# Two score blocks under way on VectorE, and 196 blocks in place of 172, in a gated mix of two attentions

## The chip, the cores and the metric

The kernel runs on one core of a Trainium2 chip. The metric is the device time of one execution in microseconds (us). The engines of a core work side by side, each through a queue of its own in program order: TensorE (PE, matmuls), VectorE (DVE), ScalarE (ACT), GpSimd (POOL) and SyncE (SP, which issues DMAs).

## The reference

For `x` of 2048 x 512 (bf16), two attentions are computed and mixed by a gate per row. A is full attention with 32 heads of 16; B looks at 8 earlier rows, two apart.

```python
g = sigmoid((x * gate_w).sum(-1, keepdims=True))
# A: full attention
q, k, v = split(x @ wqkv)                       # 32 heads of 16
p = softmax(einsum("bhqd,bhkd->bhqk", q, k) * 16 ** -0.5)
a = einsum("bhqk,bhkd->bhqd", p, v).merge_heads() @ wo
# B: the same, but each query sees rows s, s-2, ..., s-14 only (masked below 0)
b = local_attention(x, B_wqkv, B_wo)
out = g * a + (1 - g) * b
```

## The kernel before

**Full attention (A).** The work is cut into 32 periods, each one of 4 chunks of 512 queries and one of 8 groups of four heads. The periods run over the chunks in pairs: first all groups of the chunks 0 and 1, then those of 2 and 3. A period has 64 score blocks, 16 tiles of 128 keys for each of four heads; a block has 128 keys by 512 queries. TensorE computes the scores into PSUM (`qk`, tile `ring`), ScalarE exponentiates two or three blocks by one instruction (`ex`, from `ring` into `pT`), and TensorE multiplies them with the values and accumulates (`pv`, tile `acc`). A column of ones beside the values gives the sum for the division. At the end of a period VectorE transposes `acc` (`accT`), takes the reciprocal (`rden`), and GpSimd divides.

**Blocks on VectorE.** In each period the first `n_dve[pi]` blocks of the list `dorder` (the last two key tiles) are not given to ScalarE: VectorE computes an approximate exponential with integer arithmetic on the bits. These are 172 of 2048 blocks. `d_group` makes them, two by two. For each block `chain_of` issues `dq` (two matmuls into one bank `misc`: a constant term from `off`, then the scores) and four passes over 128 x 512 on VectorE: `p1` writes `dt` from the scores, `p2` and `p3` write `dt` again from the scores and `dt`, `p4` writes the result into `pd`. Then `pv` of the group multiplies both blocks with the values. There is one buffer `dt`, so that a block's four passes come to an end before the next block's first. `pd` holds two blocks, with three buffers. The matmuls `dq` of a block come after the start of the last pass (`d_last`) of the block before.

**PSUM.** `ring` has two sets of banks (three and two). Three banks, `misc0` to `misc2`, serve everything else: the accumulators, all projections, the outputs and the blocks for VectorE.

**Around it.** TensorE also does the projections of A, period by period, and those of B; VectorE evacuates them. Attention B runs mostly on GpSimd, from tiles that DMAs fetch with shifted rows. `zero` issues matmuls with zeros (`z`, tile `z32`) into `acc`, which change no sum and fill TensorE's gaps.

**What sets the order.** Every step is an `Op` with an engine, an assumed duration `occ`, a due time `dl`, its predecessors (`deps` wait for an end, `after` for a start) and the buffers it takes and uses (`tok`). `list_schedule` plays the steps through and always takes, of those that can start on an engine, the one with the earliest due time; `AHEAD` says how far it looks past the first, and `slack` is a margin that it leaves behind a step of VectorE or GpSimd before TensorE or GpSimd uses the result. The steps are then issued in that order, engine by engine, and keep it on the chip. `CFG` holds the parameters; the due times of a period come from `S0 = T0 + UNIT * (blocks before it)`. Nearly all instructions are recorded by one helper, so the profile has one line for them (L285, matmuls L297) and they are told apart by their tiles.

Of the kernel before, what the change touches and what calls it, by code (L numbers as in the profile page):

```python
# [9 lines left out]
ALU = mybir.AluOpType  # L10
# [3 lines left out]
U16 = mybir.dt.uint16  # L14
# [2 lines left out]

CFG = dict(
    set_sizes=(3, 2),
    n_dve=(3,) * 2 + (5,) * 14 + (6,) * 16,  # L20
    dve_tiles=2,
    p_bufs=4,
    pairs=True,
    cover=0.68,
    force=1.0,
    d_slack=2.0,
    d_lead=4.0,
    d_early=5.0,
    dq_early=10.0,
    d_late=8.0,  # L30
    pd_bufs=3,
    q_bufs=3,
    shift=6.0,
    hold=0.3,
    pv_dl=2.2,
    first=0.0,
    same=2.0,
    step=2,
    early=0.25,
    a_slack=0.6,  # L40
    v_slack=0.3,
    g_slack=4.0,
    unit=0.461,
    t0=18.5,
    b_start=32.0,
    b_space=46.7,
    chain=("pe", "dve", "act", "pool", "sp"),
)
# [58 lines left out]
class Op:  # L107

    def __init__(self, eng, occ, fn, dl, deps=(), alloc=(), use=(), lat=None, rel=0.0, name="",
                 after=(), rows=False, cover=None, slack=None, sums=()):  # L110
        self.eng, self.occ, self.fn, self.dl, self.rel, self.name = eng, occ, fn, dl, rel, name
        self.rows, self.zeros, self.spare = rows, 0, None
        self.sums = sums
        self.slack = {"dve": CFG["v_slack"], "pool": CFG["g_slack"]}.get(eng, 0.0) if slack is None else slack
        self.cover = cover if cover is not None else (occ if not callable(occ) else 0.0)
        self.after = [d for d in after if d is not None]
        self.deps, self.alloc = [d for d in deps if d is not None], list(alloc)
        self.lat = (occ if not callable(occ) else occ(0.0)) + LAT[eng] if lat is None else lat
        self.done = None
        for tk in list(alloc) + list(use):  # L120
            tk.ops.append(self)
# [3 lines left out]
WAVE = lambda n: 0.01 + 0.205 * n  # L125
TURN = 0.10
SPAN, COVER, ZERO = 3.41, CFG["cover"], 0.216
AHEAD = dict(pe=0.10, dve=0.12, act=0.25, pool=0.5, sp=0.0)


def list_schedule(ops, spare):
# [23 lines left out]
    while len(out) < len(ops):  # L155
        best = None
        for e, cs in cand.items():
            if not cs:
                continue
            es = [(max(free[e], avail(o)), o) for o in cs]  # L160
            t0 = min(x[0] for x in es)
            if t0 < INF and (best is None or t0 < best[0]):
                best = (t0, e, es)
        if best is None:
            raise RuntimeError("no op can start: " + ", ".join(o.name for cs in cand.values() for o in cs))
        t0, e, es = best
        same = CFG["same"] if e == "pe" else 0.0
        t, o = min(((t, o) for t, o in es if t <= t0 + AHEAD[e]),
                   key=lambda x: (x[1].dl - (same if x[1].rows == rows else 0.0), x[0]))
        if e == "pe" and not o.name.startswith("qk"):  # L170
            nxt = min(((ts, x) for ts, x in es if x.name.startswith("qk") and ts < t0 + CFG["hold"]), default=None,
                      key=lambda x: x[0])
            if nxt is not None:
                due = max(nxt[0], free["act"] - nxt[1].lat - CFG["early"])

                def ends(t, x):
                    return t + x.occ + (TURN if x.rows != rows else 0.0) + (0.0 if x.rows else TURN)
                if ends(t, o) > due + 0.03:
                    fits = [(t, x) for t, x in es if t <= t0 + AHEAD[e] and ends(t, x) <= due + 0.03]
                    t, o = min(fits, key=lambda x: (x[1].dl, x[0])) if fits else nxt  # L180
        occ = o.occ(t) if callable(o.occ) else o.occ
        lat = o.lat
        if e == "pe":
            closed = not any(0 < n < full for n, full in sums.values())
            recent = [x for x in recent if x[0] > t - SPAN]
            turn = TURN if o.rows != rows else 0.0
            lack = COVER * SPAN - sum(x[1] for x in recent) - o.cover
            if lack > 0 and t > free[e] and recent:
                turns = 2 * TURN if o.rows and rows else 0.0
                o.zeros = max(0, min(int(lack / ZERO) + 1, int((t - free[e] - turns + 0.04) / ZERO)))  # L190
            late = 0.0
            if lack - o.zeros * ZERO > CFG["force"] * ZERO and recent and not (o.rows and rows):
                o.zeros += 1
                late = ZERO
            if o.zeros and closed:
                if not any(tk.res is spare for tk in o.alloc) and max(spare.avail(True), free[e]) + o.zeros * ZERO + (2 * TURN if o.rows else 0.0) <= t + late + 0.05:
                    o.spare = Tok(spare)
                    o.spare.ops.append(o)
                    spare.take(o.spare, t)
                else:  # L200
                    o.zeros, late = 0, 0.0
            if o.zeros:
                recent.append((t - 0.1, o.zeros * ZERO))
            for key, n, full in o.sums:
                sums[key] = (sums.get(key, (full, full))[0] - n, full)
            occ, lat = occ + turn + late, lat + turn + late
            recent.append((t, o.cover))
            rows = o.rows
        for tk in o.alloc:
            tk.res.take(tk, t)  # L210
        o.t, o.end, o.done = t, t + occ, t + max(occ, lat)
        free[e] = t + occ
        cand[e].remove(o)
        out.append(o)
        for s_ in succ.get(o, ()):
            left[s_] -= 1
            if left[s_] == 0:
                s_.ready = max([s_.rel] + [d.end if d.eng == s_.eng else d.done + (d.slack if s_.eng == "pe" or d.eng == "pool" else 0.0)
                                           for d in s_.deps]
                               + [d.t for d in s_.after])  # L220
                cand[s_.eng].append(s_)
# [4 lines left out]
def kernel(  # L226
# [83 lines left out]
    def op(eng, occ, fn, dl, **kw):  # L310
        o = Op(eng, occ, fn, dl, **kw)
        ops.append(o)
        return o
# [3 lines left out]
    def tok(tag, cap):  # L317
        if tag not in res:
            res[tag] = Res(cap, tag == "misc")
        return Tok(res[tag])  # L320
# [635 lines left out]
            pi, j = max(spots, key=lambda x: (x[1] == strip[0], x[0]))  # L956
            mm(acc_tiles[pi][32 * j:32 * j + 32, :], z32[:], ones_t[:], False, False, tile_position=(0, 32 * j))

    d_last = [None]

    def d_group(pi, gr, lo, hi):
        c_, i = periods[pi]
        n = len(gr)
        st = {}
        tp = tok("pd", cfg["pd_bufs"])

        def chain_of(q_, t, j, dl):
            tx, td = tok("misc", NB), tok("dt", 1)

            def dq():  # L970
                st["x"] = ps.tile([128, QW], FP32, tag=f"misc{bank[0]}", bufs=1, name="misc")
# [3 lines left out]
                st["fr"] = st["x"][:].bitcast(U16).rearrange("p (n two) -> p n two", two=2)[:, :, 0]  # L975

            def p1():
                st["dt"] = work.tile([128, QW], FP32, name="dt", tag="dt", bufs=1)
                V.tensor_scalar(out=st["dt"][:], in0=st["fr"], scalar1=EXP_A, scalar2=EXP_C, op0=ALU.subtract, op1=ALU.mult)

            def p2():
# [4 lines left out]
                V.tensor_tensor(out=st["dt"][:], in0=st["fr"], in1=st["dt"][:], op=ALU.mult)  # L986

            def p4():
                if q_ == 0:
                    st["pd"] = work.tile([128, 2, QW], BF16, name="pd", tag="pd", bufs=cfg["pd_bufs"])  # L990
                V.tensor_tensor(out=st["pd"][:, q_, :].bitcast(U16), in0=st["x"][:], in1=st["dt"][:], op=ALU.add)
            a = op("pe", 0.43, dq, dl - 3.8 - cfg["dq_early"], rows=True, deps=[o_q[pi], o_kc[i][t // TPC] if i else o_kc0[t // TPC]],
                   after=[d_last[0]], alloc=[tx], use=[q_tok[pi]], rel=lo, lat=0.68, name=f"dq{pi}")
            a = op("dve", 0.70, p1, dl - 2.3, deps=[a], alloc=[td], use=[tx])
            a = op("dve", 0.70, p2, dl - 1.4, deps=[a], use=[td, tx])
            a = op("dve", 0.70, p3, dl - 0.7, deps=[a], use=[td, tx])
            d_last[0] = op("dve", 0.70, p4, dl, deps=[a], alloc=[tp] if q_ == 0 else [],
                           use=[td, tx] + ([tp] if q_ else []), slack=cfg["d_slack"])

        def pv():  # L1000
            for q_, (t, j) in enumerate(gr):
                pv_mm(pi, t, j, st["pd"][:, q_, :], vp_all[:, t])
        for q_, (t, j) in enumerate(gr):
            chain_of(q_, t, j, hi - 1.0 - 3.5 * (n - 1 - q_))
        a = d_last[0]
        o_pv[pi].append(op("pe", 0.23, pv, max(hi, S0[pi] + 5.0), deps=[a, o_t0[pi]] + [o_v[(4 * i + j, t)] for t, j in gr],
                           use=[tp, acc_tok[pi], acc_two[pi]], name=f"dpv{pi}",
                           sums=[((pi, j_), sum(1 for x in gr if x[1] == j_), NT) for j_ in sorted(set(x[1] for x in gr))]))

    for pi in range(NP):  # L1010
# [168 lines left out]
```

## Time and profile before

| | |
|---|---|
| time, median of 3 runs | 890.87 us (887.99 to 891.14) |
| the profiled execution | 891.62 us, span 889.8 us |
| mean granted TensorE clock | 0.988 |
| busy share of the span | PE 90%, DVE 78%, ACT 97%, POOL 70% |
| score blocks on ScalarE / VectorE | 1876 / 172 |

How to read it: the page gives the busy time of each engine, the span in 40 slices (a digit is a busy share in tenths, PEclk the granted clock), the chain of work that ended last, and groups of instructions as `out<-in xcount | busy us, mean ns of one | idle time of the engine before them, and what ended most of it`. A wait reads `engine tile <- what it waited for: us in total, times, longest`. A row of the timeline has start, duration, engine, line, operation, tiles, shapes and count, and in brackets the idle time before it.

### The profile page before, as it was taken

The page shows a single profiled execution, that of the slowest core. Times are in us where ns is not written, and L with a number is a line of the kernel's source. Part 1 is how long each engine was busy: PE and PEld are TensorE (multiplying, and loading weights), DVE is VectorE, ACT ScalarE, POOL GpSimd, SP SyncE. Part 2 cuts the span into 40 slices and gives each one's busy share as a digit, 9 for nine tenths or more (in the row PEclk, how much of TensorE's full clock was granted, in tenths as well). Part 3 has the DMA queues.
Part 4 walks back from the last instruction along what each step waited for, and adds up shares of the span by engine and source line. Part 5 has one row for each costly group of instructions (what it writes and reads, how often), then busy time and mean ns, then how long its engine had stood idle before and what let it go on. Part 6 is the DMA issues. An engine that isn't in the chain of part 4 may idle for free.

```text
span 889.8 us, 18611 instructions
## 1 busy us (share of the span) xinstructions
PE 800.3 (90%) x7472; PEld 261.5 (29%) x7472; DVE 696.3 (78%) x1121; ACT 862.7 (97%) x777; POOL 619.3 (70%) x607
## 2 busy tenths in 40 slices
PE   8989999999999999998998998898989888998985
PEld 4223332223332233222232322222222222232221
DVE  5678878887788787877668888889888886879775
ACT  4999999999999999999999999999999999999896
POOL 4266939798949994879999859897999991700000
PEclk9999999999999999999999999999999999999799
DMA  8301111103110302211121020303301110000001
GB/s 277 116 2 61 48 61 49 60 2 107 49 60 2 107 1 90 67 60 61 48 78 61 19 88 20 108 15 93 106 3 60 48 48 2 1 1 1 1 7 42
DMA packets 43998, 47.37 MB, mean 53 GB/s; under 512 B 1876, under 2 KB 41348, under 8 KB 43912
## 3 DMA queue, kind: packets, MB, share of 16 engines
q1 hardware_dynamic: 43912, 46.19, 16.2%
q8 instruction: 58, 0.95, 0.4%
q14 instruction: 28, 0.23, 0.1%
HBM read 39.86 MB, written 6.33 MB: 52 GB/s over the span
## 4 chain that ended last, share of the span: by engine, by line
ACT 65%; issue 25%; PE 6%; DMA 2%; DVE 1%; SPq 0%; DVEq 0%; ACTq 0%
ACT pT L285 65%; PE ring L297 2%; PE misc_ps L297 2%; PE acc L297 2%; ACT lg L285 1%; DMA xld<-in_A_x_dram 1%; DMA z_scr<-zrow 1%; PE misc L297 0%; DMA zrows<-z_scr 0%; PE pxt L493 0%; DVE zrow L285 0%; DVE osb L285 0%; SPq L285 0%; DVE qt L285 0%; DVE misc_ps L285 0%
## 5 line engine op out<-in xcount | busy, mean ns | idle before, releaser
L285 ACT ACTIVATE pT<-ring 128x1536 bf16<-128x1536 f32 x751 | 853.8, 1411 | 8.6 <-PE ring L297 6.3
L297 PE MATMUL ring<-qt,kt_all 32*128 32x512 bf16 x1876 | 298.6, 383 | 77.2 <-ACT pT L285 71.2
L285 POOL TENSOR_TENSOR prod<-prod 128x512 f32<-128x512 f32 (+1 forms) x208 | 240.1, 1168 | 6.3
L297 PE MATMUL acc<-pT,vp_all 128*17 128x512 bf16 (+1 forms) x1876 | 242.0, 386 | 0.2
L297 PEld LDWEIGHTS <-kt_all 32*128 32x128 bf16 x2048 | 123.6, 91 | 366.6 <-issue 349.8
L285 DVE TENSOR_SCALAR dt<-misc 128x512 f32<-128x512 uint16 x172 | 117.6, 684 | 75.5 <-PE misc L297 72.0
L285 POOL TENSOR_TENSOR prod<-ksh,qb 128x512 f32<-128x512 bf16 x128 | 144.0, 1159 | 30.5 <-DMA ksh<-kv_scr 18.8
L285 POOL TENSOR_TENSOR prod<-vsh,lg 128x512 f32<-128x512 bf16 x128 | 136.6, 1100 | 4.3 <-DMA vsh<-kv_scr 2.3
L285 DVE TENSOR_TENSOR dt<-misc,dt 128x512 f32<-128x512 uint16 x172 | 118.3, 688 | 5.0
L285 DVE TENSOR_TENSOR pd<-misc,dt 128x512 uint16<-128x512 f32 x172 | 118.2, 687 | 5.1
L285 DVE SCALAR_TENSOR_TENSOR dt<-misc,dt 128x512 f32<-128x512 uint16 x172 | 118.2, 687 | 4.9
L297 PEld LDWEIGHTS <-vp_all 128*17 128x17 bf16 (+1 forms) x2048 | 52.0, 88 | 124.8 <-issue 116.9
L297 PE MATMUL misc_ps<-xT,wtw 128*32 128x512 bf16 x1024 | 86.8, 386 | 0.0
L297 PE MATMUL acc<-ones_t,z 128*32 128x512 bf16 x206 | 71.7, 390 | 0.0
L285 POOL TENSOR_TENSOR ott<-accT,rden 128x256 bf16<-128x256 f32 x30 | 18.7, 622 | 76.2 <-DVE rden L285 76.2
L297 PE MATMUL misc_ps<-bw,xT 128*32 128x512 bf16 x768 | 66.2, 382 | 0.0
L297 PE MATMUL misc<-ones_t,off 32*128 32x512 bf16 x172 | 65.7, 382 | 0.4 <-DVE pd L285 0.4
L297 PE MATMUL misc<-qt,kt_all 32*128 32x512 bf16 x172 | 64.8, 377 | 0.0
L297 PEld LDWEIGHTS <-xT 128*32 128x32 bf16 (+1 forms) x1088 | 34.8, 96 | 29.8 <-issue 19.4
L297 PE MATMUL acc<-pd,vp_all 128*17 128x512 bf16 x172 | 40.1, 384 | 0.0
L285 POOL TENSOR_TENSOR lg<-lg,mx 128x256 f32<-128x256 f32 x16 | 10.1, 632 | 40.4 <-DVE mx L285 40.4
L285 POOL TENSOR_TENSOR lg<-lg,rr 128x256 f32<-128x256 f32 x16 | 10.1, 631 | 35.6 <-ACT pT L285 19.2
(73 smaller groups left out, 491.2 us busy)
## 6 DMA issues: line engine op xcount, KB each, us to landing
ksh<-kv_scr SPq DMA_DIRECT2D x16, 1024.0 KB, 5.5
vsh<-kv_scr SPq DMA_DIRECT2D x16, 1024.0 KB, 7.3
kv_scr<-kvs SPq DMA_DIRECT2D x16, 256.0 KB, 2.0
xld<-in_A_x_dram SPq DMA_DIRECT2D x4, 512.0 KB, 8.5
out_dram<-osb SPq DMA_DIRECT2D x16, 128.0 KB, 1.7
bw<-in_B_wqkv_dram SPq DMA_DIRECT2D x1, 1536.0 KB
wraw<-in_A_wqkv_dram SPq DMA_DIRECT2D x2, 512.0 KB, 9.6
wv<-in_A_wqkv_dram SPq DMA_DIRECT2D x1, 512.0 KB, 9.9
```

The source lines that it names most:

```text
L285: return chain_on(key, f(*a, **k))
L297: return chain(nc.tensor.matmul(out, lhsT=lhsT, rhs=rhs, start=start, stop=stop, **kw))
```

## The change

Two blocks may be under way on VectorE at once. `dt` gets a second buffer, and `pd` becomes a tile of one block with five buffers, each block taking its own. The matmuls of the next block come after the start of the second pass (`d_go`) of the block before, no longer after the start of its fourth. `n_dve` gives 196 blocks to VectorE, from 3 to 8 a period (84 in the first 16 periods, 112 in the later), where there were 3, 5 and 6 (76 and 96). In `list_schedule` an instruction of VectorE is assumed shorter by 0.085 us (`NEXT`), and one that depends on another of VectorE starts 0.117 us after the assumed end of that. Several parameters of due times and margins are set anew.

```diff
-    n_dve=(3,) * 2 + (5,) * 14 + (6,) * 16,
+    n_dve=(3, 4, 5, 8, 4, 6, 5, 6, 7, 5, 5, 4, 6, 5, 5, 6, 8, 5, 7, 7, 7, 6, 8, 7, 7, 8, 7, 7, 8, 6, 7, 7),
-    d_slack=2.0,
+    d_slack=0.5,
-    dq_early=10.0,
-    d_late=8.0,
-    pd_bufs=3,
+    dq_early=8.0,
+    d_late=10.0,
+    pd_bufs=5,
-    hold=0.3,
-    pv_dl=2.2,
-    first=0.0,
-    same=2.0,
+    hold=0.2,
+    pv_dl=3.2,
+    first=2.0,
+    same=3.0,
-    a_slack=0.6,
+    a_slack=0.8,
-    g_slack=4.0,
-    unit=0.461,
+    g_slack=2,
+    unit=0.459,
-    b_start=32.0,
+    b_start=30.0,
...
+        if eng == "dve":
+            self.occ = max(0.08, occ - NEXT)
...
-AHEAD = dict(pe=0.10, dve=0.12, act=0.25, pool=0.5, sp=0.0)
+NEXT = 0.085
+AHEAD = dict(pe=0.10, dve=0.05, act=0.25, pool=0.5, sp=0.0)
...
-                s_.ready = max([s_.rel] + [d.end if d.eng == s_.eng else d.done + (d.slack if s_.eng == "pe" or d.eng == "pool" else 0.0)
+                s_.ready = max([s_.rel] + [d.end + (0.117 if d.eng == "dve" else 0.0) if d.eng == s_.eng else d.done + (d.slack if s_.eng == "pe" or d.eng == "pool" else 0.0)
...
-        tp = tok("pd", cfg["pd_bufs"])
-
-        def chain_of(q_, t, j, dl):
-            tx, td = tok("misc", NB), tok("dt", 1)
+        blocks = []
+
+        def block(t, j, dl):
+            st = {}
+            tx, td, tp = tok("misc", NB), tok("dt", 2), tok("pd", cfg["pd_bufs"])
...
-                st["dt"] = work.tile([128, QW], FP32, name="dt", tag="dt", bufs=1)
+                st["dt"] = work.tile([128, QW], FP32, name="dt", tag="dt", bufs=2)
...
-                if q_ == 0:
-                    st["pd"] = work.tile([128, 2, QW], BF16, name="pd", tag="pd", bufs=cfg["pd_bufs"])
-                V.tensor_tensor(out=st["pd"][:, q_, :].bitcast(U16), in0=st["x"][:], in1=st["dt"][:], op=ALU.add)
+                st["pd"] = work.tile([128, QW], BF16, name="pd", tag="pd", bufs=cfg["pd_bufs"])
+                V.tensor_tensor(out=st["pd"][:].bitcast(U16), in0=st["x"][:], in1=st["dt"][:], op=ALU.add)
...
-                   after=[d_last[0]], alloc=[tx], use=[q_tok[pi]], rel=lo, lat=0.68, name=f"dq{pi}")
+                   after=[d_go[0]], alloc=[tx], use=[q_tok[pi]], rel=lo, lat=0.68, name=f"dq{pi}")
...
             a = op("dve", 0.70, p2, dl - 1.4, deps=[a], use=[td, tx])
+            d_go[0] = a
...
-            d_last[0] = op("dve", 0.70, p4, dl, deps=[a], alloc=[tp] if q_ == 0 else [],
-                           use=[td, tx] + ([tp] if q_ else []), slack=cfg["d_slack"])
+            a = op("dve", 0.70, p4, dl, deps=[a], alloc=[tp], use=[td, tx], slack=cfg["d_slack"])
+            blocks.append((st, tp, a))
```

The product `pv` of a group then waits for the last passes of all its blocks.

More of the change, by code (lines that the diff above doesn't have):

```diff
@@ L957, in zero @@
             mm(acc_tiles[pi][32 * j:32 * j + 32, :], z32[:], ones_t[:], False, False, tile_position=(0, 32 * j))
-    d_last = [None]
+    d_go = [None]
     def d_group(pi, gr, lo, hi):
@@ L963, in d_group @@
         n = len(gr)
-        st = {}
-        tp = tok("pd", cfg["pd_bufs"])
-        def chain_of(q_, t, j, dl):
-            tx, td = tok("misc", NB), tok("dt", 1)
+        blocks = []
+        def block(t, j, dl):
+            st = {}
+            tx, td, tp = tok("misc", NB), tok("dt", 2), tok("pd", cfg["pd_bufs"])
             def dq():
@@ L988, in p4 @@
             def p4():
-                if q_ == 0:
-                    st["pd"] = work.tile([128, 2, QW], BF16, name="pd", tag="pd", bufs=cfg["pd_bufs"])
-                V.tensor_tensor(out=st["pd"][:, q_, :].bitcast(U16), in0=st["x"][:], in1=st["dt"][:], op=ALU.add)
+                st["pd"] = work.tile([128, QW], BF16, name="pd", tag="pd", bufs=cfg["pd_bufs"])
+                V.tensor_tensor(out=st["pd"][:].bitcast(U16), in0=st["x"][:], in1=st["dt"][:], op=ALU.add)
             a = op("pe", 0.43, dq, dl - 3.8 - cfg["dq_early"], rows=True, deps=[o_q[pi], o_kc[i][t // TPC] if i else o_kc0[t // TPC]],
-                   after=[d_last[0]], alloc=[tx], use=[q_tok[pi]], rel=lo, lat=0.68, name=f"dq{pi}")
+                   after=[d_go[0]], alloc=[tx], use=[q_tok[pi]], rel=lo, lat=0.68, name=f"dq{pi}")
             a = op("dve", 0.70, p1, dl - 2.3, deps=[a], alloc=[td], use=[tx])
             a = op("dve", 0.70, p2, dl - 1.4, deps=[a], use=[td, tx])
+            d_go[0] = a
             a = op("dve", 0.70, p3, dl - 0.7, deps=[a], use=[td, tx])
-            d_last[0] = op("dve", 0.70, p4, dl, deps=[a], alloc=[tp] if q_ == 0 else [],
-                           use=[td, tx] + ([tp] if q_ else []), slack=cfg["d_slack"])
+            a = op("dve", 0.70, p4, dl, deps=[a], alloc=[tp], use=[td, tx], slack=cfg["d_slack"])
+            blocks.append((st, tp, a))
         def pv():
-            for q_, (t, j) in enumerate(gr):
-                pv_mm(pi, t, j, st["pd"][:, q_, :], vp_all[:, t])
+            for (t, j), (st, tp, a) in zip(gr, blocks):
+                pv_mm(pi, t, j, st["pd"][:], vp_all[:, t])
         for q_, (t, j) in enumerate(gr):
[L1004 to L1007, printed above, removed]
+            block(t, j, hi - 1.0 - 3.5 * (n - 1 - q_))
+        o_pv[pi].append(op("pe", 0.23, pv, max(hi, S0[pi] + 5.0), deps=[b[2] for b in blocks] + [o_t0[pi]] + [o_v[(4 * i + j, t)] for t, j in gr],
+                           use=[b[1] for b in blocks] + [acc_tok[pi], acc_two[pi]], name=f"dpv{pi}",
                            sums=[((pi, j_), sum(1 for x in gr if x[1] == j_), NT) for j_ in sorted(set(x[1] for x in gr))]))
```

## The prediction

> **What bounds the kernel now.** I read the page first, then the waits, then the stretches in which ScalarE stood still. The page's busy times, slices, chain and groups:
>
> ```profile
> span 889.8 us, 18611 instructions
> PE 800.3 (90%) x7472; PEld 261.5 (29%) x7472; DVE 696.3 (78%) x1121; ACT 862.7 (97%) x777; POOL 619.3 (70%) x607
> ...
> DVE  5678878887788787877668888889888886879775
> ACT  4999999999999999999999999999999999999896
> ...
> PEclk9999999999999999999999999999999999999799
> ...
> ACT 65%; issue 25%; PE 6%; DMA 2%; DVE 1%; SPq 0%; DVEq 0%; ACTq 0%
> ...
> L285 ACT ACTIVATE pT<-ring 128x1536 bf16<-128x1536 f32 x751 | 853.8, 1411 | 8.6 <-PE ring L297 6.3
> ...
> L285 DVE TENSOR_SCALAR dt<-misc 128x512 f32<-128x512 uint16 x172 | 117.6, 684 | 75.5 <-PE misc L297 72.0
> ...
> L285 DVE TENSOR_TENSOR dt<-misc,dt 128x512 f32<-128x512 uint16 x172 | 118.3, 688 | 5.0
> L285 DVE TENSOR_TENSOR pd<-misc,dt 128x512 uint16<-128x512 f32 x172 | 118.2, 687 | 5.1
> L285 DVE SCALAR_TENSOR_TENSOR dt<-misc,dt 128x512 f32<-128x512 uint16 x172 | 118.2, 687 | 4.9
> ```
>
> ScalarE is busy 97% of the span, from the second slice to the last; its exponentials over `ring` take 853.8 us and stand idle for only 8.6 us in all. VectorE is at 78%, TensorE at 90%. The groups give the exchange: the 2048 score blocks are shared between ScalarE (1876) and VectorE (172, four passes each). Every block that VectorE takes shortens the bound, as long as nothing that ScalarE needs comes late through it. The waits say who is in reserve:
>
> ```profile
> DVE dt L285 <- PE misc L297: 72.0, 79, 4.6
> PE ring L297 <- ACT pT L285: 71.2, 254, 1.0
> ```
>
> TensorE waits for ScalarE 254 times, 71.2 us together, so TensorE is ahead of the bound; and VectorE, of its 193.5 idle us (889.8 - 696.3), spends 72.0 in front of a first pass whose scores are not yet there. That is the wait that the change goes for.
>
> **The change part by part.** *ScalarE, on the path.* 24 blocks (196 - 172) leave it. Their price is the pace of an undisturbed stretch in the timeline of ScalarE:
>
> ```profile
> 621.61 50.99 ACT L285 ACTIVATE pT<-ring 128x1024 bf16<-128x1024 f32 x45
> 672.22 0.67 ACT L285 ACTIVATE lg<-lg 128x256 f32<-128x256 f32 x1
> ```
>
> 45 sets, by turns two and three blocks and so 112 blocks, take from 621.61 to 672.22: 50.61 / 112 = 0.452 us a block. 24 x 0.452 = 10.85 us. (The whole group, 853.8 / 1876 = 0.455, gives 10.9.) The sum of sets falls from 751 to 741.
>
> *VectorE, off the path so far.* Each block brings four passes of 0.687 us: 4 x 0.687 = 2.75 us, and 24 of them 66 us. Against that stands what turns save. The timeline of VectorE:
>
> ```profile
> 829.50 0.69 DVE L285 TENSOR_TENSOR pd<-misc,dt 128x512 uint16<-128x512 f32 x1
> 830.11 0.80 DVE L285 TENSOR_SCALAR qt<-misc_ps,rowq,rowl 128x512 bf16<-128x512 f32 x1
> ...
> 832.30 0.69 DVE L285 SCALAR_TENSOR_TENSOR dt<-misc,dt 128x512 f32<-128x512 uint16 x1
> 833.03 0.69 DVE L285 TENSOR_TENSOR dt<-misc,dt 128x512 f32<-128x512 uint16 x1
> 833.75 0.69 DVE L285 TENSOR_TENSOR pd<-misc,dt 128x512 uint16<-128x512 f32 x1
> ```
>
> A pass that reads what the pass just before it wrote starts 0.72 to 0.73 us after it (832.30, 833.03, 833.75). An instruction that doesn't read it (`qt` behind `pd`) starts after 0.61 us, 0.08 us before the recorded end of the other. So each pass with something unrelated in front of it is worth 0.12 us. How often is that so? In the order that the two kernels issue to VectorE, 442 of the 516 second to fourth passes stand directly behind their own forerunner before, and 340 of 588 after: 2.57 a block against 1.73. The 0.84 a block that are saved are worth 0.10 us, 20 us over 196 blocks. Only 60 of the 196 blocks begin while another is under way; "two at once" is the exception, and other VectorE work does much of the separating. Net, VectorE's work grows by about 66 - 20 = 46 us, into 193.5 us of idle time.
>
> [...]
>
> Does it fit where it is densest? The stretches:
>
> ```profile
> 600.00:700.00 100.00, 90.55 (x746) 28.46 (x746) 86.08 (x135) 100.00 (x91) 92.11 (x90) 1.00 0.21 69
> 834.00:849.00 15.00, 14.90 (x65) 2.99 (x64) 8.73 (x13) 11.96 (x12) 0.00 (x0) 0.54 0.00 0
> ```
>
> The columns after the stretch are its length, then PE, PEld, VectorE (86.08 in the first row), ScalarE, GpSimd, and the granted clock. The later 16 of 32 periods go from 96 blocks to 112, one more each; the earlier 16 from 76 to 84. A period of 58 ScalarE blocks is 58 x 0.452 = 26.2 us, so 100 us hold 3.8 periods. VectorE gets 3.8 x 2.75 = 10.5 us more there and, with some 27 blocks, 27 x 0.10 = 2.7 us less: 86.1 + 7.8 = 93.9 of the 98.3 us that the stretch then lasts (3.8 x 0.452 = 1.7 us less on ScalarE). It fits, with 4 us to spare in a hundred, where it had 14. I take nothing for it on the path; if that cover is gone, each late pass costs as below.
>
> *TensorE.* Each block moved trades one score matmul in `ring` for two in `misc` (the constant term `off` and the scores); the product with the values stays. That is 24 matmuls more, against 28 fewer fillers (`z`) in the issued order, 211 to 183. Beside 71.2 us of waiting for ScalarE I cost it at nothing; without that cover it would be 24 x 0.22, some 5 us, by the start-to-start distance of the two matmuls of a block:
>
> ```profile
> 831.16 0.37 PE L297 MATMUL misc<-qt,kt_all 32*128 32x512 bf16 x1
> ...
> 838.10 0.60 PE L297 MATMUL misc<-ones_t,off 32*128 32x512 bf16 x1
> ...
> 838.50 0.63 PE L297 MATMUL misc<-qt,kt_all 32*128 32x512 bf16 x1
> ```
>
> (here 0.40 us at the low clock of 834 to 849, half of it at full clock; the durations 0.63 and 0.37 show the two states).
>
> *Earlier issue.* The scores of the next block are ordered behind the second pass of the one before, no longer behind its fourth. That is two passes, 1.45 us, earlier, which covers the mean wait of 72.0 / 79 = 0.91 us. VectorE gains idle time, not the path.
>
> *Banks, the added wait.* Three `misc` banks serve the accumulator, all projections and these scores. A block keeps its bank from its scores to its fourth pass; two under way keep two of the three. What that can do, the trace of before already shows once, on ScalarE, VectorE and TensorE:
>
> ```profile
> 490.48 3.71 ACT L285 ACTIVATE pT<-ring 128x1536 bf16<-128x1536 f32 x3 [1.95 <-PE acc L297]
> ...
> 489.07 0.69 DVE L285 TENSOR_TENSOR pd<-misc,dt 128x512 uint16<-128x512 f32 x1
> ...
> 489.98 0.82 PE L297 MATMUL acc<-pT,vp_all 128*32 128x512 bf16 x9
> ```
>
> The first products of a new period need a bank; the fourth pass that frees it ends at 489.76, the matmuls start at 489.98, everything behind them in TensorE's queue stands, and ScalarE loses 1.95 us. One more such event is that dear.
>
> *Due times and margins* (`hold`, `pv_dl`, `first`, `same`, the slacks, `unit`): they move instructions in the order, and have no price of their own. The order's assumed VectorE costs become 0.615 us plus 0.117 behind a forerunner, close to the 0.61 and 0.72 above; before, 0.70 was assumed for every pass. `d_slack` from 2.0 to 0.5 lets TensorE come to the product sooner after the fourth pass; if VectorE is later than assumed, that is a stall between 0 and the 1.95 us above, and five single `pd` buffers for three double ones change nothing while it is not. I take 1 us off the 8.6 us of idle time in front of `ring` for the closer fit; its bounds are -8.6 (all goes) and +8.6 (doubles).
>
> *Sum.* The profiled execution took 891.62 us, its span 889.8, 1.8 lying around it. 891.62 - 10.85 - 1.0 = 879.8. The median of three runs, 890.87, is 0.75 below that execution; so **879.0 us** for the median.
>
> **The rivals.**
>
> *Banks and VectorE's late passes decide* (it ends slower). With 94% of the later half filled and two banks held, stalls like that at 490 come at the turns of periods, where two accumulators are alive. For: the one row above, and three banks as before. Against: 31 turns gave only one clear case. At 1.95 us, 10.85 / 1.95, about 6 more eat the gain; from (10.85 + 4.5) / 1.95, about 8 more, it is slower by over 0.5%. At every second turn: 880.0 + 16 x 1.95 = 911 us; at every fourth it is 896. Chance of over 8: 0.08; of 3 to 8 (886 to 895 us): 0.05.
>
> *The turns buy nothing.* The passes stay at 0.72 us, so the later half gets 86.1 + 10.5 = 96.6 of 98.3 us, before any wait of VectorE for TensorE; half of the present rate of 72.0 us in 890, 4 us in 100, wouldn't fit, 2.3 us too much. Over the 428 us of the later half, 16 x 26.7, that is 10 us: 879.0 + 10 = 889 us. Against: the rows of 0.61. Chance 0.05. It is also the case of a change that doesn't do what it says, since only 60 blocks overlap. [...]
>
> *Low clock.* From 834 to 849 the granted clock was 0.54, matmuls took 0.60 to 0.63 instead of 0.37, and ScalarE was busy for 11.96 of 15.00 us: 3.0 us lost, without VectorE. The fillers are there against this, and there are 28 fewer of them. Three such stretches more than now: 879.0 + 9 = 888 us, chance 0.05; none at all: 876. The Trainium skill's page "TensorE: Matmul & The Clock Gate" (section "HAM oscillation") asks for no idle gap of over 3.4 us; this stretch has no such gap (PE busy 14.90 of 15.00) and was slow.
>
> *All stalls go*: the 8.6 us vanish with the 10.85: 891.62 - 19.45 - 0.75 = 871.4 us. For: an order closer to VectorE's true pace. Against: the low clock stays. Chance 0.07.
>
> **How the numbers follow.** My forecast, 874 to 884 us, has 0.70. The range runs from the case without stalls, 872, to the case with the idle time doubled, 879.0 + 1 + 8.6, 888; it takes in the forecast, most of the low clock and part of the middle cases. A measurement of this kernel can tell about 0.5%, 4.5 us, from no change (the three runs span 3.15 us): faster is below 886.4, slower above 895.3. Faster: 0.70 + 0.07 and about half of the low clock and of the few bank stalls, 0.05, with a little of the turns that buy nothing, 0.02: 0.84. Same: 0.08. Slower: 0.08.
>
> **What would show it.** Right: 740 or 741 exponentials, about 843 us busy; idle before them not over 8.6 us; the wait of `dt` for TensorE well below 72.0 us; VectorE busy some 740 us, around 94 in the densest 100 us; neighbouring passes at 0.61 us where the blocks take turns. Wrong: idle time in front of `ring` of 15 us or more with `acc` or `pd` as releaser (banks), passes at 0.72 us although another block's stands between (turns), a clock below 0.9 in more than two slices (low clock). The forecast falls if ScalarE's pace of 0.452 us changes, which nothing in this change touches.

## The result, and the profile after

The changed kernel takes **877.65 us** (median of 4 runs, 877.14 to 878.37), the one before 889.43 us in the same comparison (4 runs, 886.96 to 891.14). The ratio is 0.987, 95% interval 0.9841 to 0.9899: 1.3% faster. The forecast was 879.0 us in a range of 872 to 888. (Here and below, ratios leave out executions over 1.5% above the fastest of their kernel; medians do not.)

The page of the changed kernel: span, busy times, slices of VectorE, ScalarE and the granted clock, and the groups of the exponentials and of the four passes (lines have moved by three, L285 to L288 and L297 to L300).

```profile
span 875.9 us, 18559 instructions
PE 795.0 (91%) x7468; PEld 257.9 (29%) x7468; DVE 735.4 (84%) x1217; ACT 852.1 (97%) x767; POOL 619.3 (71%) x607
...
DVE  6488888898899788976869899988988998798996
ACT  5999999999999999999999999999999999999995
...
PEclk9999999999999999999999999999999999999998
...
L288 ACT ACTIVATE pT<-ring 128x1536 bf16<-128x1536 f32 x741 | 843.0, 1393 | 6.4 <-PE ring L300 6.1
...
L288 DVE TENSOR_SCALAR dt<-misc 128x512 f32<-128x512 uint16 x196 | 133.9, 683 | 44.4 <-PE misc L300 42.6
...
L288 DVE TENSOR_TENSOR dt<-misc,dt 128x512 f32<-128x512 uint16 x196 | 134.1, 684 | 4.8
L288 DVE SCALAR_TENSOR_TENSOR dt<-misc,dt 128x512 f32<-128x512 uint16 x196 | 134.2, 684 | 4.0
L288 DVE TENSOR_TENSOR pd<-misc,dt 128x512 uint16<-128x512 f32 x196 | 133.6, 681 | 2.8
```

ScalarE is still the bound, at 97%. The profiled execution took 877.70 us against 891.62, 13.92 less. The exponentials give 853.8 - 843.0 = 10.8 of it in busy time and 8.6 - 6.4 = 2.2 in idle time. The remaining 0.9 lies ahead of them: the first exponential starts at 18.44 us (ScalarE's timeline), where it started at 19.40.

```profile
18.44 6.88 ACT L288 ACTIVATE pT<-ring 128x1536 bf16<-128x1536 f32 x6 [1.56 <-PE ring L300]
```

VectorE went from 696.3 to 735.4 us, and the wait of the first pass for its scores from 72.0 to 42.6 us.

The passes in turn, from VectorE's timeline of the changed kernel:

```profile
666.39 0.69 DVE L288 SCALAR_TENSOR_TENSOR dt<-misc,dt 128x512 f32<-128x512 uint16 x1
667.12 0.69 DVE L288 TENSOR_TENSOR dt<-misc,dt 128x512 f32<-128x512 uint16 x1
667.73 0.68 DVE L288 TENSOR_SCALAR dt<-misc 128x512 f32<-128x512 uint16 x1
668.32 0.68 DVE L288 TENSOR_TENSOR pd<-misc,dt 128x512 uint16<-128x512 f32 x1
668.92 0.68 DVE L288 SCALAR_TENSOR_TENSOR dt<-misc,dt 128x512 f32<-128x512 uint16 x1
669.63 0.69 DVE L288 TENSOR_TENSOR dt<-misc,dt 128x512 f32<-128x512 uint16 x1
```

The third pass at 667.12 stands 0.73 us behind the second, which it reads. Then the next block's first pass comes in between (667.73), and three instructions follow each other at 0.59 to 0.61 us, up to the next dependent one (669.63, 0.71 behind). Every pass is recorded with the same 0.68 or 0.69 us; the difference is in the starts alone.

ScalarE's pace in an undisturbed stretch, and the densest 100 us of the prediction (VectorE is the third figure after the length):

```profile
632.11 51.43 ACT L288 ACTIVATE pT<-ring 128x1536 bf16<-128x1536 f32 x45
683.29 0.55 ACT L288 ACTIVATE lg<-lg 128x256 f32<-128x256 f32 x1
```

```profile
600.00:700.00 100.00, 89.82 (x755) 27.08 (x748) 90.91 (x150) 100.00 (x92) 94.45 (x92) 1.00 0.17 51
```

45 sets, here 113 blocks, take 51.18 us, 0.453 us a block as before. VectorE is at 90.9 where 93.9 was expected.

### The profile page after: what moved, and what is told of

The parts are those of the page before. It is cut to its first block, busy times and chain, and to the rows that moved or that the text cites. A ratio compares the mean times of both kernels' runs of the same rounds, so it can differ in the third digit from the quotient of the medians.

```text
span 875.9 us, 18559 instructions
## 1 busy us (share of the span) xinstructions
PE 795.0 (91%) x7468; PEld 257.9 (29%) x7468; DVE 735.4 (84%) x1217; ACT 852.1 (97%) x767; POOL 619.3 (71%) x607
## 4 chain that ended last, share of the span: by engine, by line
ACT 66%; issue 25%; PE 7%; DVE 1%; DMA 1%; DVEq 0%; ACTq 0%
ACT pT L288 65%; PE misc_ps L300 3%; PE ring L300 2%; PE acc L300 2%; ACT lg L288 1%; DMA z_scr<-zrow 1%; PE pxt L496 1%; PE misc L300 0%; DVE zrow L288 0%; DVE osb L288 0%; ACT kt_all L288 0%; DVEq L1176 0%; DVE misc_ps L288 0%; DVE qt L288 0%; DVE accT L288 0%
## 5 line engine op out<-in xcount | busy, mean ns | idle before, releaser
L288 ACT ACTIVATE pT<-ring 128x1536 bf16<-128x1536 f32 x741 | 843.0, 1393 | 6.4 <-PE ring L300 6.1
L300 PE MATMUL ring<-qt,kt_all 32*128 32x512 bf16 x1852 | 295.9, 383 | 70.4 <-ACT pT L288 62.5
L288 POOL TENSOR_TENSOR prod<-prod 128x512 f32<-128x512 f32 (+1 forms) x208 | 240.0, 1169 | 6.3
L300 PE MATMUL acc<-pT,vp_all 128*17 128x512 bf16 (+1 forms) x1852 | 239.3, 387 | 1.0 <-ACT pT L288 0.7
L300 PEld LDWEIGHTS <-kt_all 32*128 32x128 bf16 x2048 | 119.1, 91 | 354.3 <-issue 334.8
L288 POOL TENSOR_TENSOR prod<-ksh,qb 128x512 f32<-128x512 bf16 x128 | 144.0, 1158 | 38.5 <-DMA ksh<-kv_scr 34.6
L288 DVE TENSOR_SCALAR dt<-misc 128x512 f32<-128x512 uint16 x196 | 133.9, 683 | 44.4 <-PE misc L300 42.6
L288 POOL TENSOR_TENSOR prod<-vsh,lg 128x512 f32<-128x512 bf16 x128 | 136.7, 1102 | 2.5 <-DMA vsh<-kv_scr 0.5
L288 DVE TENSOR_TENSOR dt<-misc,dt 128x512 f32<-128x512 uint16 x196 | 134.1, 684 | 4.8
L288 DVE SCALAR_TENSOR_TENSOR dt<-misc,dt 128x512 f32<-128x512 uint16 x196 | 134.2, 684 | 4.0
L288 DVE TENSOR_TENSOR pd<-misc,dt 128x512 uint16<-128x512 f32 x196 | 133.6, 681 | 2.8
L300 PEld LDWEIGHTS <-vp_all 128*17 128x17 bf16 (+1 forms) x2048 | 52.2, 88 | 127.5 <-issue 119.4
L300 PE MATMUL misc_ps<-xT,wtw 128*32 128x512 bf16 x1024 | 82.8, 384 | 0.0
L300 PE MATMUL misc<-ones_t,off 32*128 32x512 bf16 x196 | 74.9, 382 | 0.2 <-DVE osb L288 0.2
L300 PE MATMUL misc<-qt,kt_all 32*128 32x512 bf16 x196 | 73.8, 376 | 0.0
L300 PE MATMUL misc_ps<-bw,xT 128*32 128x512 bf16 x768 | 67.6, 391 | 0.0
L300 PE MATMUL acc<-ones_t,z 128*32 128x512 bf16 x179 | 63.7, 392 | 0.0
L288 POOL TENSOR_TENSOR ott<-accT,rden 128x256 bf16<-128x256 f32 x30 | 18.7, 623 | 57.1 <-DVE rden L288 57.1
L288 POOL TENSOR_TENSOR lg<-lg,mx 128x256 f32<-128x256 f32 x16 | 10.1, 631 | 48.4 <-DVE mx L288 48.4
L300 PEld LDWEIGHTS <-xT 128*32 128x32 bf16 (+1 forms) x1088 | 34.8, 96 | 28.8 <-issue 18.8
L300 PE MATMUL acc<-pd,vp_all 128*17 128x512 bf16 x196 | 42.3, 383 | 0.0
L288 POOL TENSOR_TENSOR lg<-lg,rr 128x256 f32<-128x256 f32 x16 | 10.1, 630 | 36.8 <-DVE rr L288 22.7
```

Source lines behind the costliest of these rows:

```text
L288: return chain_on(key, f(*a, **k))
L300: return chain(nc.tensor.matmul(out, lhsT=lhsT, rhs=rhs, start=start, stop=stop, **kw))
```

## The experiments

All were run against the kernel before, whose median was 889 to 890 us in each comparison. "Overlap" is the number of blocks that begin while another is under way, and "direct" the number of second to fourth passes that stand directly behind their own forerunner, both in the issued order. The ratio is to the kernel before.

| run | blocks | overlap | direct | median us | ratio, 95% interval |
|---|---|---|---|---|---|
| before | 172 | 0 | 442 of 516 | 889.43 | |
| after | 196 | 60 | 340 of 588 | 877.65 | 0.987 (0.9841 to 0.9899) |
| blocks alone | 196 | 0 | 499 of 588 | 946.59 | 1.0628 (1.0593 to 1.0663) |
| after, 172 blocks | 172 | 38 | 327 of 516 | 889.13 | 1.0007 (0.9986 to 1.0027) |
| after, one dt buffer | 196 | 0 | 437 of 588 | 896.54 | 1.008 (1.0053 to 1.0107) |
| after, old margins and costs | 196 | 14 | 461 of 588 | 904.3 | 1.0177 (1.0126 to 1.0227) |
| after, old margins | 196 | 65 | 341 of 588 | 897.85 | 1.0036 (0.9995 to 1.0077) |
| after, old costs | 196 | 9 | 457 of 588 | 914.14 | 1.0286 (1.0249 to 1.0322) |
| after, scores behind fourth pass | 196 | 0 | 433 of 588 | 945.33 | 1.0645 (1.0593 to 1.0697) |
| after, 209 blocks | 209 | 70 | 357 of 627 | 887.11 | 0.9995 (0.9963 to 1.0027) |
| old margins, more filler | 196 | 52 | 348 of 588 | 892.39 | 1.003 (0.9997 to 1.0063) |
| after, no fillers | 196 | 69 | 333 of 588 | 948.01 | 1.0638 (1.0588 to 1.0688) |
| after, even spread | 196 | 62 | 338 of 588 | 894.62 | 1.0014 (0.9971 to 1.0057) |
| after, 184 blocks | 184 | 49 | 336 of 552 | 891.88 | 1.002 (0.9986 to 1.0054) |

**The blocks alone.** The kernel before, with nothing but the new `n_dve`.

```diff
-    n_dve=(3,) * 2 + (5,) * 14 + (6,) * 16,
+    n_dve=(3, 4, 5, 8, 4, 6, 5, 6, 7, 5, 5, 4, 6, 5, 5, 6, 8, 5, 7, 7, 7, 6, 8, 7, 7, 8, 7, 7, 8, 6, 7, 7),
```

> The kernel before with the new distribution of 196 blocks alone: one block at a time, one dt buffer, the old margins and assumed costs. Theory (the count of ScalarE's blocks sets the time, VectorE has room): the 24 blocks are worth 10.85 us here too, 878 to 881 us; idle time in front of ring near the 8.6 us of before. Rival (without turns VectorE is over-full, 196 blocks need two under way): VectorE's passes come late for the accumulator, ScalarE idles 15 us or more, 885 to 892 us.

946.59 us: 57 us slower than before, against 8 to 11 us faster. The busy time of the exponentials fell as expected (842.8 us), but their idle time rose to 70.7. Most of it is in a few places. The largest, in ScalarE's and TensorE's timelines, and the busy times in it:

```profile
864.67 5.97 ACT L285 ACTIVATE pT<-ring 128x1536 bf16<-128x1536 f32 x5 [28.63 <-PE acc L297]
...
836.09 0.39 PE L297 MATMUL ring<-qt,kt_all 32*128 32x512 bf16 x2 [0.20 <-ACT pT L285]
...
864.17 0.82 PE L297 MATMUL acc<-pT,vp_all 128*32 128x512 bf16 x10
...
866.17 0.39 PE L297 MATMUL ring<-qt,kt_all 32*128 32x512 bf16 x3 [0.52 <-ACT pT L285]
```

```profile
836.00:864.00 28.00, 22.13 (x217) 8.58 (x216) 26.41 (x40) 0.04 (x1) 0.00 (x0) 1.00 0.00 1
```

For 30 us no scores for ScalarE are made. The first products of the new period (864.17) stand in TensorE's queue behind the scores of eight of VectorE's blocks, one after another, with the output projections among them; VectorE is busy for 26.41 of the 28 us and ScalarE for 0.04, at full clock. So VectorE is the bound there, although it is at 80% over the whole span. The limit of two open accumulators (`acc_two`) is not what holds the products back: VectorE had transposed the accumulator of two periods earlier at 830.06 us, so that one alone was open during the stall (VectorE's timeline).

```profile
830.06 0.71 DVE L285 STREAM_TRANSPOSE accT<-acc 128x512 f32<-128x512 f32 x1
```

What they lack is a bank: of the three, one holds the open accumulator, and the other two go by turns to blocks and projections with earlier due times, each kept until VectorE has worked through it. That is where VectorE's lag is paid. (The profile doesn't number the banks; this is read from the order that the code makes.) The stall is planned: `list_schedule`, played through, has a pause of 32.9 us between the exponentials at this place and ends its last step at 943.3 us.

**After with 172 blocks.** `n_dve` of before in the kernel after.

> The kernel after with the old distribution of 172 blocks: two under way, all margins and assumed costs as after. Theory: the blocks are the gain, so it loses 24 x 0.452 = 10.85 us against after: 887 to 890 us, that is before less 0 to 2 us. Rival (the order and the closer costs are the gain): 884 us or less.

889.13 us, no change from before. Turns, margins and assumed costs bring nothing by themselves. Against after, 24 blocks are worth 11.5 us. VectorE waits longer for scores here than the 72.0 us of before, although they are ordered earlier:

```profile
L288 DVE TENSOR_SCALAR dt<-misc 128x512 f32<-128x512 uint16 x172 | 117.6, 684 | 85.8 <-PE misc L300 84.6
```

**One dt buffer.**

```diff
-            tx, td, tp = tok("misc", NB), tok("dt", 2), tok("pd", cfg["pd_bufs"])
+            tx, td, tp = tok("misc", NB), tok("dt", 1), tok("pd", cfg["pd_bufs"])
...
-                st["dt"] = work.tile([128, QW], FP32, name="dt", tag="dt", bufs=2)
+                st["dt"] = work.tile([128, QW], FP32, name="dt", tag="dt", bufs=1)
```

> The kernel after with one dt buffer, so that no block's first pass comes before the fourth of the one in front; 196 blocks, margins and costs as after. Theory: VectorE loses about 0.1 us a block, 20 us of work, into idle time it has: 878 to 881 us. Rival (turns carry the gain): 885 us or more, with VectorE's passes as releasers in front of TensorE.

896.54 us, the rival's side, but not by its sign: of TensorE's waits for VectorE none is longer than 2.4 us. The profiled execution was the fastest of its runs (890.37 us); its exponentials idle for 17.9 us, and the longest single wait for an accumulator is 4.4 us:

```profile
L288 ACT ACTIVATE pT<-ring 128x1536 bf16<-128x1536 f32 x741 | 843.5, 1374 | 17.9 <-PE acc L300 9.3
...
ACT pT L288 <- PE acc L300: 9.3, 4, 4.4
```

**Margins and assumed costs of before.** `CFG` of before except `n_dve` and `pd_bufs`; `NEXT`, the 0.117 us and `AHEAD["dve"]` undone.

> The kernel after with two dt and five pd buffers, the next block's scores behind the second pass, 196 blocks, but the due times, margins and assumed VectorE costs of before. Theory: margins only shift the order, worth the 1 to 2 us of idle time: 878 to 881 us. Rival (they carry the gain): 885 us or more.

904.3 us. The order then overlaps 14 blocks, and stalls of the same kind as above appear, the largest again at an accumulator (ScalarE's timeline):

```profile
821.90 9.14 ACT L288 ACTIVATE pT<-ring 128x1536 bf16<-128x1536 f32 x8 [13.31 <-PE acc L300]
```

The two next runs separate margins from costs.

**Old margins, new costs.**

> The kernel after with the due times and margins of before, but the new assumed VectorE costs (0.085 us off each, 0.117 behind a forerunner). Theory, as the first four runs left it (24 blocks are worth 10.85 us only while VectorE closes each period's accumulator in time, and it does by taking turns, which the assumed costs put into the order: 65 blocks begin while another is under way, 341 of 588 passes directly behind their own): 878 to 883 us. Rival (the due times and margins make the room): 890 us or more, near the 904 us of both undone.

897.85 us in the median, as the rival said, but for the most part not for its reason: the runs follow the granted clock (below), from 885.17 us upwards. At equal clock the old margins cost 8 us.

**New margins, old costs.** Only `NEXT`, the 0.117 us and `AHEAD["dve"]` undone.

> The kernel after with the new due times and margins, but the old assumed VectorE costs; the order then overlaps 9 blocks, and 457 of 588 passes stand directly behind their own. Theory (turns make the room): 890 us or more, stalls in front of ring with acc as releaser. Rival (margins make the room): 878 to 883 us.

914.14 us. With 9 overlaps the turns are gone although their buffers are there: it is the assumed costs that make `list_schedule` put another block's pass between two dependent ones. The planner, which takes VectorE's passes for longer here, ends at 920.0 us itself; no run separates the missing turns from what else this changes in the order.

**Scores behind the fourth pass.**

```diff
             a = op("dve", 0.70, p2, dl - 1.4, deps=[a], use=[td, tx])
-            d_go[0] = a
...
             a = op("dve", 0.70, p4, dl, deps=[a], alloc=[tp], use=[td, tx], slack=cfg["d_slack"])
+            d_go[0] = a
```

> The kernel after with the next block's scores ordered behind the start of the fourth pass again, as before; two dt buffers, costs and margins as after. No block overlaps another then; 433 of 588 passes stand directly behind their own. Theory (turns make the room): as with one dt buffer, 890 to 900 us, and VectorE waits for scores 70 us or more instead of 42.6. Rival (other VectorE work between the passes is enough, or the dt buffer is what counts): 885 us or less.

945.33 us, far beyond the 890 to 900 of the theory. The first passes and their waits:

```profile
L288 DVE TENSOR_SCALAR dt<-misc 128x512 f32<-128x512 uint16 x196 | 134.9, 688 | 126.6 <-PE misc L300 124.3
...
DVE dt L288 <- PE misc L300: 124.3, 119, 7.1
```

Three times the wait of after, from one line. The two parts hang together: without early scores the second `dt` buffer brings no overlap. But the early scores do more than make turns possible: the kernel with one `dt` buffer has no overlap either, and with early scores it takes 896.54 us, 49 less.

**209 blocks.** One more in every second period, up to 8.

> The kernel after with 209 blocks, one more in every second period, up to 8. Theory (VectorE is near its end at 196: 91 of 100 us busy in the densest stretches, four passes of 0.61 to 0.72 us more each): the 13 x 0.452 = 5.9 us are lost again in stalls, 877 to 890 us. Rival (VectorE has room in its 140 idle us): 871 to 873 us.

887.11 us: the 5.9 us are lost and more. The exponentials idle for 20.4 us (6.4 in after), VectorE is busy for 769.2 of 885.1 us.

**More filler with the old margins.** The run with old margins and new costs, `cover=0.8` in place of 0.68.

> As the run with old margins and new costs (low clock for 100.4 us of its profile, 161 fillers in its order), but cover at 0.80 for 0.68, which puts 368 fillers into the order. Theory (that run lost its gain to the low clock): low clock under 40 us and 880 to 888 us. Rival (it lost it to late passes of VectorE): low clock goes, the time stays at 893 us or more.

892.39 us, between theory and rival. The worst runs are gone (nine lie between 888.79 and 898.47 us, granted clock 0.970 to 0.985), the best are no better. Fillers narrow the spread of the clock, but with the old margins they don't give the time of after. The tenth execution, the profiled one, was of another kind (last section), so no profile explains this run.

**No fillers in after.**

```diff
-                o.zeros = max(0, min(int(lack / ZERO) + 1, int((t - free[e] - turns + 0.04) / ZERO)))
+                o.zeros = 0 * max(0, min(int(lack / ZERO) + 1, int((t - free[e] - turns + 0.04) / ZERO)))
...
-                o.zeros += 1
-                late = ZERO
+                pass
```

> The kernel after without the fillers that the order puts into TensorE's gaps (184 matmuls down to 1; the sums are unchanged). Theory (the fillers hold the clock, and a low clock starves ScalarE): low clock for 100 us or more, 895 to 930 us. Rival (TensorE at 91% busy holds its clock by itself): low clock as after, about 25 us, 876 to 880 us.

948.01 us, beyond the theory's 930. 183 matmuls that compute nothing are worth 70 us. The granted clock was 0.843 to 0.851 in the undisturbed runs. The score matmuls for ScalarE, mean 433 ns where they were 383, and one stretch (clock at the end before the DMA share, ScalarE fourth after the length):

```profile
L299 PE MATMUL ring<-qt,kt_all 32*128 32x512 bf16 x1852 | 337.8, 433 | 82.6 <-ACT pT L287 77.5
...
734.00:761.00 27.00, 26.59 (x132) 4.92 (x132) 21.25 (x35) 22.14 (x19) 18.38 (x18) 0.50 0.15 47
```

At half clock ScalarE is busy for 22.14 of 27 us, with 21.25 of VectorE: TensorE, busy for 26.59, is the bound there.

**196 blocks spread evenly.** `n_dve=(3,) * 2 + (5,) * 6 + (6,) * 8 + (7,) * 16`.

> The kernel after with its 196 blocks spread evenly: 3, 3, six times 5, eight times 6, sixteen times 7 (84 and 112 in the halves, as after). Theory (a period's accumulator closes late where VectorE has much else): a few stalls in front of ring more, 880 to 890 us. Rival (only the sum matters): 876 to 880 us.

894.62 us, beyond the theory; the runs, 883.22 to 897.0, again follow the clock. The best of them is 6 us behind after.

**184 blocks.** One fewer in the twelve fullest periods.

> The kernel after with 184 blocks, one fewer in the twelve fullest periods. Theory (ScalarE's count sets the time at or below 196): 877.65 + 12 x 0.452 = 883 us, 881 to 885. Rival (196 already stalls, so fewer are no worse): 879 us or less.

891.88 us, where both sides expected at most 885. Fewer blocks than after, more than before, and no faster than before.

**What the spread of the runs shows.** In the executions of one kernel the time follows the mean granted clock closely. The kernel before, over the 63 executions in the comparisons with these runs: 886.05 us at 0.997, 890.41 at 0.990, 896.03 at 0.978, which is 5.0 us for each 0.01 by a straight line (correlation -0.97). The even spread: 883.22 at 0.982 and 896.34 at 0.956, also 5.0. Old margins with new costs: 885.17 at 0.988, 897.96 at 0.963, 5.1. The run without fillers fits the same rate: after at 0.987 and 877.65, and 0.14 less clock, make 877.65 + 70 = 948. So part of what separates the kernels is their clock, and lines through each kernel's own runs (those that the ratios count), read at 0.987, take it out. The last column has the end of the last step when `list_schedule` plays the kernel through; the durations that it assumes are the same at every granted clock.

| kernel | at clock 0.987, us | planned end, us |
|---|---|---|
| before (172) | 891.7 | 884.2 |
| after, 172 blocks | 889.8 | 883.8 |
| after, 184 blocks | 885.2 | 881.4 |
| after (196) | 877.6 | 872.7 |
| after, even spread (196) | 880.4 | 875.9 |
| after, 209 blocks | 881.6 | 878.5 |
| after, old margins (196) | 886.0 | 881.2 |
| after, one dt buffer (196) | 887.4 | 884.4 |

(The values of 209, of the even spread and of one `dt` buffer lie a little outside their runs, whose highest clock was 0.982.) At equal clock the blocks do bring their price: 172, 184, 196 give 889.8, 885.2, 877.6, that is 12.2 us for 24. The planned ends lie 3 to 8 us below these times. They contain the large stalls (943.3 us for the blocks alone, 920.0 for the old costs, 941.7 for the scores behind the fourth pass), and nothing of what the fillers are worth (876.2 without them, against 948.01 measured). So the large stalls come with the order and could have been read from it beforehand.

After also had a steady clock, 0.987 or 0.988 in its four runs, where the even spread has 0.956 to 0.982 and 184 blocks 0.963 to 0.986, in ten runs each of another comparison. Four runs of one comparison don't show that its order is what keeps the clock, and why one order should keep it and another not was not isolated. The profile with old margins and new costs, one of the slowest executions of that kernel, shows only how little idle time goes ahead of a fall (TensorE's timeline, then a stretch):

```profile
549.30 0.39 PE L300 MATMUL ring<-qt,kt_all 32*128 32x512 bf16 x3 [0.95 <-ACT pT L288]
...
551.61 0.60 PE L300 MATMUL ring<-qt,kt_all 32*128 32x512 bf16 x3 [0.40 <-ACT pT L288]
```

```profile
551.00:562.00 11.00, 10.60 (x63) 2.04 (x61) 8.22 (x14) 8.44 (x9) 3.81 (x5) 0.53 0.29 97
```

In the 8 us ahead of the fall the longest idle time of TensorE is 0.95 us. Then matmuls take 0.60 us for 0.39, ScalarE is busy for 8.44 of 11 us, and the clock stands at 0.53. (The Trainium skill's page "TensorE: Matmul & The Clock Gate", section "HAM oscillation", names idle gaps of over 3.4 us as what brings the low clock. No such gap stands here.)

## Why the prediction was right

**ScalarE's share: right.** 10.85 us were worked out, 10.8 are gone from the busy time; the pace of 0.452 us held (0.453).

**The idle time: mis-sized.** I took 1 us off, within -8.6 and +8.6; it was 2.2. The start of the exponentials, 0.96 us earlier, wasn't in the sum at all. Together they are why the profiled execution came out at 877.70, 2.1 us below the 879.8 of the sum.

**VectorE: the sum right, the cover wrongly reasoned.** Busy some 740 us was forecast, 735.4 measured, and in the densest stretch 93.9 against 90.9. The starts of 0.61 and 0.72 us held (0.59 to 0.61, 0.71 to 0.73). But I then called the saved 20 us idle time and gave them no price in the sum. The step that fails is "It fits, with 4 us to spare in a hundred, where it had 14. I take nothing for it on the path": after itself bears it out, but it does not follow from the busy share. With one `dt` buffer the kernel takes 896.54 us, 19 more than after (10 at equal clock), though VectorE's busy time there, 748.8 us, is only 13 more. The busy share of a long stretch did not tell whether VectorE is done with the banks in time for each new period. My rival "the turns buy nothing", at 889 us, has VectorE's room run out in this way; the run that takes the turns away lies 8 us above it in the median, and 2 us below it at equal clock.

**Earlier scores: wrong for the path.** The wait fell by 29.4 us, as said, but not by the early scores alone: with 172 blocks and the same early scores it is 84.6 us. What they bring shows where VectorE is full: "VectorE gains idle time, not the path" is refuted by the 945.33 us without them, with a wait of 124.3 us.

**Margins: wrong.** They "have no price of their own", I wrote: undone with the costs they take the gain and 15 us more (904.3), the costs alone 914.14, the margins alone 897.85 in the median (886.0 at equal clock). The order is what those numbers make, and the large stalls are already in the order.

**Banks and late passes: place right, price wrong.** The rival put stalls at the turns of periods and priced each at 1.95 us, by the only row of before. Where they came, they took 13.31 us (old margins and costs) and 28.63 us (the blocks alone). Few such stalls, not the eight that I asked for, turn the sign. In after none of that kind is left: 6.1 of the 6.4 us idle are in front of `ring`.

**Low clock: the price about right, the chance far too low.** 3.0 us for 15 us at 0.54 was the row; such a stretch takes 0.008 off the mean clock, which is 3.9 us by the 5 us for 0.01 that separate the runs of one kernel. I gave 0.05 to a kernel with more of it; six of the nine other 196-block kernels had a mean clock below 0.97 in some run. In after one such stretch looks like this (ScalarE's timeline, then the stretch):

```profile
112.09 1.02 ACT L288 ACTIVATE pT<-ring 128x1024 bf16<-128x1024 f32 x1 [1.07 <-PE ring L300]
```

```profile
109.00:113.00 4.00, 4.00 (x24) 0.94 (x21) 2.66 (x5) 2.93 (x3) 1.75 (x4) 0.57 0.00 0
```

So the number came out because all parts of the change were there together, each of which I had priced at nearly nothing. That was in part luck: the same reckoning gave 878 to 881 us with one `dt` buffer, and with the old margins and costs, and those kernels took 896.54 and 904.3. The two turns of the argument that carried it were ScalarE's pace and that the idle time would not grow. The first is shown; the second was argued from a sum that the neighbours of this kernel disprove. No version beat after.

## What to carry to other kernels

When work moves from the bound to an engine at 80%, the saved time on the bound is easily read, but a busy share doesn't show whether the other engine meets each deadline: look for the buffers that both need (here three banks for accumulators, projections and blocks), and count what has to be done before one comes free, period by period. Where a planner writes the order, the costs it assumes are part of the kernel; set them by the start-to-start distances of the trace, dependent and independent apart, and read the planned end first: most of these kernels could have been told apart by it. And compare variants at equal granted clock, or they are ranked by the clock.

## What the runs showed of the hardware that was not expected

The recorded duration of these passes is no measure of what they take of the engine: 0.68 to 0.69 us in the rows above, while the successor starts after 0.59 to 0.61 us or, if it reads the result, after 0.71 to 0.73.

The time is sensitive to the clock although TensorE isn't the bound on the average: 5 us for each 0.01 of mean clock.

In two executions, one of the ten with more filler and one of the four without fillers, the kernel took 3692.47 and 1203.35 us, at a recorded clock of 1.00. The first was profiled:

```profile
span 3690.4 us, 18924 instructions
...
L300 PE MATMUL ring<-qt,kt_all 32*128 32x512 bf16 x1852 | 1127.2, 1433 | 1.8 <-ACT pT L288 1.8
```

The score matmuls took 1433 ns for 383, and the weight loads beside them 140 ns for 91, while VectorE's four passes took 682 to 692 ns, much as in the other runs. The cause wasn't found, and the ratios leave both executions out.
